# One expert slot picked inside attention and run unsplit during the routing

## The chip, the cores and the metric

The kernel runs on one core of one Trainium2 chip. The metric is the time of one execution on the device, in microseconds. Engines are named as in the profile: PE is TensorE's matrix product, PEld its weight load, DVE VectorE, ACT ScalarE, POOL GpSimd and SP the engine that issues most transfers.

## The reference, cut to what matters

```
q, k, v: (4, 8, 576, 64)                    # fp32
scores = rotate(q) @ rotate(k).T / sqrt(64)
attn_out = softmax(scores) @ v              # (4, 8, 576, 64)
x = attn_out.transpose(0, 2, 1, 3).reshape(2304, 512)

xn = x / (norm(x) + 1e-6);  en = emb / (norm(emb) + 1e-6)       # emb: (8, 512)
logits = xn @ en.T / tau
expert_idx = argmax(logits, axis=1)
gate_w = softmax(logits)[expert_idx]
for e in range(8):                          # w1: (8, 512, 1024), w2: (8, 1024, 512)
    mask = expert_idx == e
    out[mask] = gate_w[mask] * (relu(x[mask] @ w1[e]) @ w2[e])

h = out @ w_in                              # (512, 2048), float64
g = h - tanh(h)
return g @ w_out                            # (2048, 512), float64
```

## The kernel before, in words

**Stages.** The kernel has four stages, one after the other. Attention goes over 16 pairs of heads, four pairs to a batch. Then the rows are routed to the experts. Then the experts work on slots of rows. Then a dense layer of two products with a curve between works on six groups of 384 rows.

**Attention.** The order of attention's work is a list of some 1,200 steps written out by hand (`ORDER`, a string): `sm3.1` is "scores of pair 3, row block 1", `ld`, `ro`, `pp`, `ph`, `pl`, `sk` prepare q and k, `sx`, `se` are maximum and exponential, `tp`, `to` the transposes of the probabilities, `av` the product with v (L283), `xp` a product that gives normalised rows and logits (L293), `us` the logits of a batch, `sq` the squares of a row block and `st` the store of a batch's rows to `xscr` in HBM. The steps `cl` to `cs` convert the float64 `w_in` to fp32 beside attention (class `Convert`). Each engine has a queue of its own and takes its steps in the order of the list. The rope of q and k is POOL's, the products with v and `xp` are fp32 products, all other large products are of a high and a low fp32r part (three products in place of one).

**Routing** (`route`). When all logits are there, DVE makes a one-hot table `hot` of 8 experts by 20 row blocks (L491 to L500). Two products with a triangle and with ones count it (`cr`, L504). A chain of some 30 small DVE operations works out how many slots of 256 rows (big) or 128 rows (small) each expert takes, and the position of each row. ScalarE makes 8 of the 20 tables `row` by way of `lane` and `away` (L564 to L567), DVE the other 12, and 20 small products (`inv`, L574) turn positions into a list of rows per slot, `rt.idx`. Filler transposes (`idle`, L61, 64 and 24 of them) follow on TensorE after the counting and after the listing products. POOL then gathers the rows of the first slot from `xscr` (L830).

**Experts** (`Experts.run`, `block`, `small`). Slot 1 comes first, slots 2 to 7 follow always (`ALWAYS` = 8), further big slots and the small ones only where the registers say so, and slot 0 comes last. A block makes 8 groups of 12 products for the hidden rows (`hp`, L861), takes them through ReLU into a high and a low part (`ht`, L866 and L868), and makes two groups of 24 products for the output rows (`yp`, L882). Beside them ScalarE and DVE split the next weights into parts (`wh` and `wl`, `w1h` and `w1l`, L822 and L825). The rows of `y` are scattered to `yscr` in HBM. PSUM holds three banks each for `hp` and `yp`. The weights of a slot are loaded only where its expert differs from the one before. A list `steps` of bookkeeping (the scatter positions `rows`, the gates, 20 scatters of gates) is taken up at given places `f` of the blocks.

**Conversion of `w_out`.** In blocks 1 to 7, `Convert.step` runs at f = 1, 4 and 7 (blocks 1 to 4) or at f = 2 and 6: 18 steps, of which 16 load a piece. The clamp and the mask of a piece are DVE's (L742, L744), joining the halves is DVE's (L749), the addition is POOL's (L754), and a split writes two parts to HBM.

Of the kernel before, what the change touches and what calls it, by code (L numbers as in the profile page):

```python
# [30 lines left out]
ALWAYS, NBIG, NSMALL = 8, 12, 8  # L31
NSLOT = NBIG + NSMALL
R_FRESH, R_COUNT, R_SMALL, R_FIRST = 20, 40, 41, 42
# [5 lines left out]
PRE = 8  # L39
# [3 lines left out]
IDLE = (40, 64, 24)  # L43
# [20 lines left out]
def attention(tc, ctx, q, k, v, tables, emb, tau, ident, xscr, lg, us, ss, zero, conv):  # L64
    nc = tc.nc
    st = ctx.enter_context(tc.tile_pool(name="att_static", bufs=1))
    r_p = ctx.enter_context(tc.tile_pool(name="att_rope", bufs=1))
# [10 lines left out]
    tab = st.tile([128, 4, 5, D], F32, name="tab")  # L78
    raw = {n: [st.tile([128, 2, 5, D], F32, name=f"raw_{n}{i}") for i in range(RAW_BUFS[n])] for n in "qkv"}
# [37 lines left out]
    cv = Convert(tc, ctx, *conv, ROOM, zero)  # L117
# [9 lines left out]
    def rope(i, n):  # L127
        c = 0 if n == "q" else 2
        x = raw[n][i % RAW_BUFS[n]]
        if i == 0 or (i == 1 and n == "q"):  # L130
            eng = nc.vector
            w = pt_p.tile([128, 4, 2, S], F32, tag="pt", name="early", bufs=2).rearrange("p z a b -> p (z a b)")
            ra, rb = (w[:, 640 * y:640 * y + 640].rearrange("p (h r d) -> p h r d", h=2, r=5) for y in range(2))
        else:
            eng = nc.gpsimd
            ra, rb = (r_p.tile([128, 2, 5, D], F32, tag=y, name=y) for y in ("ra", "rb"))
# [8 lines left out]
        r = r_p.tile([128, 5, 2, D], F32, tag="rot" + n, name="rot" + n, bufs=2)  # L145
# [221 lines left out]
    for i in range(NP):  # L367
        nc.gpsimd.memset(ib[i][:, 128:144], 0.0)
        nc.gpsimd.tensor_copy(ib[i][:, 0:128], ident)

    do = dict(
        ld=load, ro=rope, pp=prep_pe, ph=prep_hi, pl=prep_lo, sk=stacks, sm=s_pe, sx=s_max, se=s_exp, tp=pt_pe, to=pt_out,
# [3 lines left out]
    turn_nothing(nc, ps_o, "o", ident, IDLE[0])  # L376
# [11 lines left out]
sa ro0.k sp ro0.q pp0.1 pp0.0 pp0.2 ph0.1 ph0.0 ph0.2 pl0.1 sd pl0.0 pl0.2 ld0.v ld1.k ld1.q cl0 ld2.q ld2.k ld1.v  # L388
cl1 ep2 ep3 sm0.0 ep0 sm0.1 ed3 sx0.0 ed0 ed2 sx0.1 se0.0 se0.1 ep1 sm0.2 sm0.3 sx0.2 ed1 sx0.3 se0.2 ro1.k se0.3
sm0.4 tp0.0.3 tp0.0.2 tp0.0.1 sm0.5 sx0.4 ro1.q sx0.5 to0.0.3 se0.4 to0.0.2 to0.0.1 tp0.0.0 pp1.1 to0.0.0 ph1.1  # L390
pp1.2 pp1.0 sm0.7 ph1.2 ph1.0 cc0 se0.5 sm0.6 pl1.1 pl1.2 pl1.0 sx0.7 cb0 sx0.6 cd0 cc1 se0.7 se0.6 ca0 ld3.k ld3.q
sk1.0 ro2.k ro2.q ce0 ro3.k ro3.q sm0.8 kp0 tp0.1.1 sm1.8 tp0.1.0 sx0.8 ko0 to0.1.1 sx1.8 to0.1.0 se0.8 up0.0 se1.8
uo0.0 tp0.1.2 sm1.0 up0.1 sm1.1 tp0.1.3 to0.1.2 sx1.0 sx1.1 to0.1.3 uo0.1 se1.0 se1.1 pp2.0 pp2.1 sm1.3 pp2.2 sm1.2
ph2.2 ph2.0 ph2.1 sx1.3 sx1.2 pl2.0 pl2.1 pl2.2 av0.0 up1.0 ld4.k cl2 sk1.1 ld4.q cs0 sk2.0 se1.3 se1.2 ca1 uo1.0
ca2 ao0.0 cc2 tp1.0.2 sm1.4 sm1.5 tp1.0.0 up1.1 av0.1 cb1 cd1 sx1.4 sx1.5 cb2 cd2 ce1 ro4.q ce2 ro4.k uo1.1 to1.0.2
se1.4 se1.5 to1.0.0 ao0.1 sm1.7 sm1.6 xp0.0 tp1.0.1 tp1.0.3 sx1.7 sx1.6 xd0.0 se1.7 se1.6 to1.0.3 to1.0.1 sm2.0
sm2.1 kp1 tp1.1.0 xp0.1 sx2.0 sx2.1 ko1 to1.1.0 xd0.1 cl3 ld5.q ld2.v sk2.1 cs1 cl4 ld5.k se2.0 se2.1 sm2.2 tp1.1.1
# [12 lines left out]
to4.1.2 to4.1.0 sx5.8 to4.1.1 sx5.0 up4.0 tp4.1.3 up4.1 se5.8 uo4.0 uo4.1 se5.0 ao3.1 sm5.2 kp4 to4.1.3 sx5.2 ko4  # L410
tp4.0.3 tp4.0.2 sm5.1 xp3.0 sx5.1 xd3.0 to4.0.3 se5.2 to4.0.2 se5.1 pp6.0 sm5.3 pp6.2 sm5.4 pp6.1 ph6.2 ph6.0 ph6.1
# [63 lines left out]
def route(tc, ctx, rt, cst, us, ps, idle):  # L475
# [23 lines left out]
    for b in range(B):  # L499
        v.memset(hot[64:128, :, 5 * b + 4], 0.0)  # L500
# [876 lines left out]
```

## Time and profile before

| What | Value |
|---|---|
| Median of 3 runs | 1028.66 us (1026.74 to 1039.12) |
| The profiled execution | 1032.44 us |
| Its span, first to last instruction | 1030.7 us |
| Mean granted TensorE clock | 0.977 of 2.4 GHz |
| PE busy | 977.6 us (95%) |
| DVE busy | 833.6 us (81%) |
| ACT busy | 652.0 us (63%) |
| POOL busy | 472.0 us (46%) |

Times within the kernel are microseconds from the start of the span. The mean length of a product says how long one is under way, not how far apart two of them follow: products are pipelined, so a distance is read from starts. In a timeline the bracket at the end of a line holds how long the engine stood idle before it and what released it. A granted clock of 1.00 is 2.4 GHz, of 0.50 it is 1.2 GHz.

### The profile page before, as it was taken

The page shows a single profiled execution, that of the slowest core. Times are in us where ns is not written, and L with a number is a line of the kernel's source. Part 1 is how long each engine was busy: PE and PEld are TensorE (multiplying, and loading weights), DVE is VectorE, ACT ScalarE, POOL GpSimd, SP SyncE. Part 2 cuts the span into 40 slices and gives each one's busy share as a digit, 9 for nine tenths or more (in the row PEclk, how much of TensorE's full clock was granted, in tenths as well). Part 3 has the DMA queues.
Part 4 walks back from the last instruction along what each step waited for, and adds up shares of the span by engine and source line. Part 5 has one row for each costly group of instructions (what it writes and reads, how often), then busy time and mean ns, then how long its engine had stood idle before and what let it go on. Part 6 is the DMA issues. An engine that isn't in the chain of part 4 may idle for free. (4 is left out here: it accounts for less than half of the span.)

```text
span 1030.7 us, 18144 instructions
## 1 busy us (share of the span) xinstructions
PE 977.6 (95%) x6004; PEld 854.2 (83%) x6004; DVE 833.6 (81%) x1472; ACT 652.0 (63%) x1466; POOL 472.0 (46%) x494
## 2 busy tenths in 40 slices
PE   8899999999996899999998799999999999999994
PEld 7787888888785788888986689999999999999993
DVE  6999888889677899898668659978878788788783
ACT  3677877877764577676566457655555656555661
POOL 5656656744301354544216435544444444443432
PEclk8899999999999899999999899999999999999998
DMA  6799889887714569979458397000100100000000
GB/s 192 170 225 233 209 225 218 223 200 179 188 46 144 200 173 286 316 198 232 133 180 271 133 296 277 31 31 1 31 31 1 59 4 31 31 1 1 31 1 31
DMA packets 98623, 140.75 MB, mean 137 GB/s; under 512 B 15945, under 2 KB 65097, under 8 KB 98002
## 3 DMA queue, kind: packets, MB, share of 16 engines
q1 hardware_dynamic: 92896, 123.40, 44.3%
q0 software_dynamic: 5440, 15.75, 4.5%
q8 instruction: 51, 0.84, 0.3%
q14 instruction: 58, 0.48, 0.2%
q10 hardware_dynamic: 178, 0.28, 0.1%
HBM read 101.11 MB, written 27.55 MB: 125 GB/s over the span
## 5 line engine op out<-in xcount | busy, mean ns | idle before, releaser
L1098 PE MATMUL dh<-yt,dwh 128*128 128x384 f32 x768 | 195.7, 335 | 0.0
L1098 PEld LDWEIGHTS dh<-yt,dwh 128*128 128x128 f32 x768 | 141.7, 188 | 8.3 <-DVE yt L1087 0.2
L1128 ACT ACTIVATE gh<-e 128x384 fp32r<-128x384 f32 x96 | 50.4, 525 | 144.5 <-DVE e L1121 144.5
L1108 POOL TENSOR_SCALAR e<-z 128x384 f32<-128x384 f32 x96 | 49.6, 517 | 189.8 <-DVE gl L1131 137.4
L236 ACT ACTIVATE p<-s,nm 128x576 f32<-128x576 f32 x144 | 106.5, 742 | 43.3 <-DVE nm L223 42.1
L1098 PE MATMUL dh<-yt,dwl 128*128 128x384 f32 x384 | 130.2, 339 | 0.0
L223 DVE TENSOR_REDUCE nm<-s 128x1 f32<-128x576 f32 x144 | 106.4, 752 | 26.7 <-PE s L218 22.7
L861 PE MATMUL hp<-xt,w1h 128*128 128x256 f32 x576 | 112.5, 297 | 14.4 <-DVE ht L868 8.6
L1155 PE MATMUL dy<-dwh,gh 128*128 128x512 f32 x288 | 114.8, 398 | 4.4 <-ACT gh L1128 2.6
L1155 PE MATMUL dy<-dwl,gh 128*128 128x512 f32 x288 | 114.5, 398 | 0.0
L1120 DVE SCALAR_TENSOR_TENSOR e<-q,e 128x384 f32<-128x384 f32 x96 | 111.0, 1156 | 3.4
L1155 PE MATMUL dy<-dwh,gl 128*128 128x512 f32 x288 | 113.7, 395 | 0.0
L861 PEld LDWEIGHTS hp<-xt,w1h 128*128 128x128 f32 x576 | 95.6, 201 | 17.6 <-DVE ht L868 10.1
L1109 POOL TENSOR_TENSOR e<-e,z 128x384 f32<-128x384 f32 x96 | 102.1, 1063 | 8.0
L1131 DVE TENSOR_TENSOR gl<-e,gh 128x384 fp32r<-128x384 f32 x96 | 54.3, 565 | 56.1 <-ACT gh L1128 55.5
L882 PE MATMUL yp<-wh,ht 128*128 128x512 f32 x288 | 90.9, 397 | 0.0
L218 PE MATMUL s<-ak 128*128 128x288 f32 x480 | 89.2, 314 | 1.2 <-ACT p L236 0.6
L861 PE MATMUL hp<-xt,w1l 128*128 128x256 f32 x288 | 85.0, 295 | 0.0
L825 DVE TENSOR_TENSOR wl<-raw,wh 128x512 fp32r<-128x512 f32 x84 | 65.0, 779 | 15.6 <-ACT wh L822 13.5
L218 PEld LDWEIGHTS s<-ak 128*128 128x128 f32 x480 | 67.6, 189 | 10.2 <-ACT p L236 4.5
L1121 DVE COPY_PREDICATED e<-m,t 128x384 f32<-128x384 int32 x96 | 72.3, 753 | 3.4
L249 PE MATMUL pt_ps<-ident,p 128*128 128x128 f32 x512 | 72.2, 278 | 0.5 <-DVE pt L125 0.4
(258 smaller groups left out, 2354.8 us busy)
## 6 DMA issues: line engine op xcount, KB each, us to landing
raw<-moe_w SPq DMA_DIRECT2D x176, 256.0 KB
ak<-hl SPq DMA_DIRECT2D x30, 448.0 KB
ak<-hl SPq DMA_DIRECT2D x30, 320.0 KB
c<-moe_w_in SPq DMA_DIRECT2D x16, 512.0 KB
c<-moe_w_out SPq DMA_DIRECT2D x16, 512.0 KB
raw_k<-k SPq DMA_DIRECT2D x16, 256.0 KB
raw_q<-q SPq DMA_DIRECT2D x16, 256.0 KB
raw_v<-v SPq DMA_DIRECT2D x16, 256.0 KB
```

What stands on the lines that cost most here:

```text
L218: nc.tensor.matmul(t[:, j, 0:HALF], lhsT=x[:, c:c + 128], rhs=x[:, k:k + HALF], start=(n == 0), stop=(n == len(parts) - 1))
L223: nc.vector.tensor_reduce(out=nm, in_=ps["s", i, u][:, :, 0:HALF], op=ALU.max, axis=AX.XY, negate=True)
L236: nc.scalar.activation(out=p.rearrange("p (j c) -> p j c", j=2), in_=ps.pop(("s", i, u))[:, :, 0:HALF], func=AF.Exp, bias=ps.pop(("nm", i, ...
L249: nc.tensor.transpose(t[:, r * 128:(r + 1) * 128], prob[i, r][:, 640 * h + 128 * kt:640 * h + 128 * kt + 128], ident)
L825: self.nc.vector.tensor_tensor(out=self.wl[m, c], in0=self.raw[m, c], in1=self.wh[m, c].bitcast(F32), op=ALU.subtract)
L861: nc.tensor.matmul(hp[:, 0:W], lhsT=a[1, f][:, kk * 128:(kk + 1) * 128], rhs=xt[b][:, kk, :], start=(n == 0), stop=(n == 3 * KD - 1))
L882: nc.tensor.matmul(yp, lhsT=ht[x][:, f, cs], rhs=b[2, f], start=(f == 0 and n == 0), stop=(f == KF - 1 and n == 2))
L1098: nc.tensor.matmul(h, lhsT=a[1, f][:, kk * 128:(kk + 1) * 128], rhs=self.yt[j][b][:, kk, :], start=(n == 0), stop=(n == 3 * KD - 1))
L1109: nc.gpsimd.tensor_tensor(out=e, in0=e, in1=z, op=ALU.mult)
L1120: v.scalar_tensor_tensor(out=e, in0=q, scalar=G_B, in1=e, op0=ALU.add, op1=ALU.mult)
L1121: v.copy_predicated(e, m.bitcast(I32), t)
L1155: self.nc.tensor.matmul(self.acc[j][a], lhsT=g[x][:, cs], rhs=b[2, f], start=(f == 0 and n == 0), stop=(f == self.KF - 1 and n == 2))
```

## The change

Attention's list now also holds the steps of one "early" slot. When the logits of the first three batches are there, DVE makes their part of the one-hot table, counts it, picks the expert with most rows and takes its first 256 rows (`mv14.0` to `mv14.12`, `mc14`, `mr14`, `ml14`). SP loads that expert's w1 and w2 (`mw15.0` to `mw15.15`), POOL gathers the rows (`mg14`), TensorE and ScalarE transpose them (`mp15`, `mo15`). The hidden and output products of this slot are unsplit fp32 products: two groups of hidden products stand before the counting product of the routing, six after it, one half of the output products before the transposes of the first block's rows, the other half after them. The filler transposes of the routing are gone. The rows taken are struck from `hot`, and `ALWAYS` falls from 8 to 7. The rest of the list is arranged anew from its first line on.

The weights and rows of the early slot lie in buffers that attention and the conversions use too: `rows` is one tile of 24 x 5 x 64 words that holds q, k, the rope's products and tables as views; `conv` and `cx` hold both conversions' pieces. In the conversion of `w_out` the clamp moves from DVE to POOL, the mask moves to the next step, and each of blocks 1 to 6 takes three steps. The PSUM pools after attention wait by tile.

```diff
-ALWAYS, NBIG, NSMALL = 8, 12, 8
+ALWAYS, NBIG, NSMALL = 7, 12, 8
+EARLY = (2, 6)
+EB = B - 1
+ET = 5 * EB
+A_ROPE, A_TAB, A_RAW, A_ROT, A_ROWS = 0, 4, 8, 16, 24
...
-    raw = {n: [st.tile([128, 2, 5, D], F32, name=f"raw_{n}{i}") for i in range(RAW_BUFS[n])] for n in "qkv"}
+    raw = {n: [early.pair(A_RAW, 2 * y + i) for i in range(RAW_BUFS[n])] for y, n in enumerate("qk")}
...
-            ra, rb = (r_p.tile([128, 2, 5, D], F32, tag=y, name=y) for y in ("ra", "rb"))
+            ra, rb = (early.pair(A_ROPE, y) for y in range(2))
...
+class Early:
+    def __init__(self, tc, ctx, rt, cst, us, xscr, yscr, w1, w2, ident):
...
+        self.rows = p.tile([128, A_ROWS, 5, D], F32, name="rows")
+        self.conv = p.tile([128, 6, 512], F32, name="conv")
+        cx = p.tile([128, 3, 513], F32, name="cx")
...
+    def steps(self, lg, bank):
...
+        def rows(i):
+            for t in range(ET):
+                g.tensor_scalar(out=row[t], in0=rt.iota, scalar1=lane[:, t:t + 1], scalar2=None, op0=ALU.is_equal)
+
+        def list_pe(i):
+            t = held["inv"] = bank()
+            for z in range(ET):
+                nc.tensor.matmul(t[:, 0:2], lhsT=row[z], rhs=col[:, z], start=(z == 0), stop=(z == ET - 1))
...
+    def up(self, f, ps):
+        nc = self.nc
+        hp = ps.tile([128, 512], F32, tag="h", name="eh")[:, 0:W]
+        for k in range(self.KD):
+            nc.tensor.matmul(
+                hp.rearrange("p (r d) -> p r d", r=4), lhsT=self.wv[0][f][:, k // 2, k % 2 * 128:k % 2 * 128 + 128],
+                rhs=self.x[:, 4 * k:4 * k + 4], start=(k == 0), stop=(k == self.KD - 1))
+        return lambda: nc.scalar.activation(out=self.h[f], in_=hp.rearrange("p (r d) -> p r d", r=4), func=AF.Relu)
+
+    def down(self, a, ps):
+        nc = self.nc
+        yp = ps.tile([128, 512], F32, tag="y", name="ey")
+        for f in range(self.KF):
+            nc.tensor.matmul(
+                yp.rearrange("p (h d) -> p h d", h=2), lhsT=self.h[f][:, 2 * a:2 * a + 2], rhs=self.wv[1][f],
+                start=(f == 0), stop=(f == self.KF - 1))
...
 def route(tc, ctx, rt, cst, us, ps, ps_h, early):
...
+    for x in pick(nc, rt, cst, us, sc, m2, ET, NT):
+        x()
+    for f in range(EARLY[0]):
+        early.up(f, ps_h)()
     cr = ps.tile([128, 512], F32, tag="t", name="cr")
...
-    idle(IDLE[1])
...
     nc.gpsimd.tensor_tensor(out=rank, in0=inc, in1=suf, op=ALU.add)
+    for f in range(EARLY[0], EARLY[1]):
+        early.up(f, ps_h)()
+    relus = [early.up(f, ps_h) for f in range(EARLY[1], Early.KF)]
...
     nc.scalar.activation(out=row[:, ac:], in_=away[:, ac:], func=AF.Relu, scale=-1.0, bias=1.0)
+    for x in relus:
+        x()
...
-    idle(IDLE[2])
...
     def clamp(self, n):
...
-        self.nc.vector.tensor_scalar(
+        eng = self.nc.gpsimd if self.late else self.nc.vector
+        eng.tensor_scalar(
             out=self.pad, in0=x.bitcast(F32), scalar1=least, scalar2=most, op0=ALU.max, op1=ALU.min)
+        if not self.late:
+            self.shift(n)
+
+    def shift(self, n):
+        x = self.xs[n % len(self.xs)]
         self.nc.vector.tensor_scalar(
             out=x, in0=self.pad.bitcast(I32), scalar1=0x07FFFFFF, scalar2=3, op0=ALU.bitwise_and, op1=ALU.logical_shift_left)
...
         if 0 < n <= len(self.jobs):
+            self.shift(n - 1)
             self.join(n - 1)
             self.add(n - 1)
...
-            if conv and f in ((1, 4, 7) if s <= 4 else (2, 6)):
+            if conv and f in (1, 4, 7):
                 conv.step()
...
-        if PRE == 8:
-            for a in range(2):
-                self.x_in(xg[a], a)
-            registers()
-        steps.insert(0, rows)
+        out = [early.down(0, self.ps_y)]
+        for a in range(2):
+            self.x_in(xg[a], a)
+        out[0]()
+        out.append(early.down(1, self.ps_y))
+        registers()
+        steps[0:0] = [out[1], rows]
...
-            self.block(s, None, conv, steps, range(6) if s == 1 else (1, 3, 5, 6))
+            self.block(s, None, conv, steps, range(7) if s == 1 else (1, 3, 5, 6))
```

The last lines of attention's list, before and after, show where the early steps stand:

```
...to15.1.2 xp14.0 up15.0 up15.1 av15.0 uo15.0 uo15.1 ao15.0 us2
xd14.0 xp14.1 av15.1 ao15.1 xp15.0 xp15.1 xd14.1 xd15.0 xd15.1 us3 us0 sq3.0 st3 sq3.1 sq3.2 sq3.3 sq3.4
```

```
...sk15.0 sk15.1 cs15 mw15.0 mw15.1 mw15.2 mw15.3 mw15.4 mw15.5 mw15.6 mw15.7 mw15.8 ld15.v mw15.9 mr14 sm14.7 xp12.1
...uo15.1 uo15.0 ao15.0 xd14.0 av15.1 xp14.1 ao15.1 xp15.0 xp15.1 xd14.1 xd15.0 xd15.1 us3 mv14.11 mv14.12 sq3.0
mw15.10 mw15.11 mw15.12 mw15.13 st3 mw15.14 mw15.15 sq3.1 sq3.2 sq3.3 sq3.4
```

## Rows read from the trace of the kernel before

**Rows 1.** The busy table of the page: engine, busy us, share, instructions.

```profile
PE 977.6 (95%) x6004; PEld 854.2 (83%) x6004; DVE 833.6 (81%) x1472; ACT 652.0 (63%) x1466; POOL 472.0 (46%) x494
```

**Rows 2.** Busy time by stretch: length, engines, granted clock, transfers' share, GB/s.

```profile
12.00:40.00 28.00, 23.65 (x127) 20.70 (x125) 22.74 (x41) 14.13 (x35) 19.58 (x16) 0.76 0.59 149
40.00:255.00 215.00, 213.44 (x1675) 175.74 (x1674) 189.86 (x381) 171.91 (x440) 131.74 (x108) 1.00 0.87 216
...
285.00:313.80 28.80, 28.75 (x223) 22.27 (x222) 18.42 (x44) 15.39 (x38) 0.78 (x6) 1.00 0.12 30
313.80:338.30 24.50, 14.49 (x119) 13.11 (x118) 19.56 (x60) 13.10 (x31) 4.86 (x6) 0.87 0.57 160
338.30:368.50 30.20, 27.41 (x154) 24.74 (x155) 28.13 (x87) 17.21 (x36) 9.82 (x8) 0.88 0.58 198
368.50:494.50 126.00, 120.02 (x762) 108.35 (x761) 109.60 (x183) 88.84 (x180) 61.73 (x53) 0.99 0.90 243
417.30:444.30 27.00, 25.09 (x154) 22.81 (x153) 23.40 (x39) 18.47 (x37) 13.37 (x11) 0.94 1.07 301
...
494.50:517.90 23.40, 23.40 (x154) 21.31 (x153) 16.82 (x30) 14.83 (x31) 6.20 (x5) 1.00 0.47 147
```

**Rows 3.** Timeline of the routing: start, length, engine, line, tiles, count, idle before.

```profile
318.42 0.43 PE L504 MATMUL cr<-hot,tri 128*128 128x160 f16 x2 [4.65 <-DVE hot L500]
...
318.64 8.70 PE L61 MATMUL idle<-ident 128*128 128x128 f32 x64
...
325.30 0.21 ACT L564 ACTIVATE lane<-ab 128x8 f32<-128x8 int32 x1 [5.59 <-DVE ab L555]
...
328.93 0.63 PE L574 MATMUL inv<-col,row 128*128 128x32 f16 x12 [0.34 <-DVE row L572]
...
334.81 0.66 PE L839 MATMUL xt_ps<-ident,xg 128*128 128x128 f32 x4 [2.59 <-DMA xg<-xscr,idx]
...
338.30 1.31 PE L861 MATMUL hp<-xt,w1h 128*128 128x256 f32 x2 [0.69 <-ACT xt L842]
```

**Rows 4.** The groups of instructions by line: the experts' products with the high part.

```profile
L861 PE MATMUL hp<-xt,w1h 128*128 128x256 f32 x576 | 112.5, 297 | 14.4 <-DVE ht L868 8.6 <-DVEq L1002 5.0 <-ACT xt L842 0.7
```

**Rows 5.** Timeline of PE, late attention: its fp32 products.

```profile
304.81 1.00 PE L293 MATMUL xo<-ib,ot 128*128 128x144 f32 x6
304.81 0.39 PE L293 MATMUL xo<-ib,ot 128*128 128x144 f32 x1
...
309.55 2.16 PE L283 MATMUL o<-pt,raw_v 128*64 128x288 f32 x16
311.54 0.66 PE L283 MATMUL o<-ptk,raw_v 128*64 128x288 f32 x4
```

**Rows 6.** Busy time by stretch, where the granted clock is half.

```profile
335.50:342.30 6.80, 4.94 (x20) 4.28 (x21) 4.40 (x25) 2.35 (x5) 5.34 (x4) 0.50 0.71 224
...
349.10:352.50 3.40, 3.40 (x16) 3.32 (x17) 3.28 (x9) 3.39 (x9) 0.47 (x1) 0.50 0.18 28
```

**Rows 7.** Timeline of block 1: the conversion's first piece, and the wait for DVE.

```profile
348.46 0.66 ACT L733 ACTIVATE cx<-c 128x512 f32<-128x512 f32 x1 [4.57 <-DMA c<-moe_w_out]
...
348.95 0.68 PE L861 MATMUL hp<-xt,w1h 128*128 128x256 f32 x2 [2.65 <-DVE ht L868]
```

**Rows 8.** Timeline of block 4, and two groups by line: splits, additions, clamps.

```profile
423.68 2.29 DVE L825 TENSOR_TENSOR wl<-raw,wh 128x512 fp32r<-128x512 f32 x1
424.13 1.28 POOL L754 TENSOR_TENSOR cx<-cx,cu 128x512 int32<-128x512 int32 x1
...
426.23 0.68 DVE L825 TENSOR_TENSOR wl<-raw,wh 128x512 fp32r<-128x512 f32 x1
426.36 0.39 PE L861 MATMUL hp<-xt,w1h 128*128 128x256 f32 x1 [1.91 <-DVE ht L868]
...
L742 DVE TENSOR_SCALAR pad<-cx 128x513 f32<-128x513 f32 x16 | 10.8, 678 | 1.8 <-ACT cx L733 1.8
L900 POOL TENSOR_SCALAR w1h<-raw 128x512 fp32r<-128x512 f32 x4 | 4.2, 1058 | 0.0
```

More of the change, by code (lines that the diff above doesn't have):

```diff
@@ L144, in rope @@
             )
-        r = r_p.tile([128, 5, 2, D], F32, tag="rot" + n, name="rot" + n, bufs=2)
+        r = early.flat(A_ROT, 2 * "qk".index(n) + i % 2).rearrange("p (r h d) -> p r h d", r=5, h=2)
         eng.tensor_tensor(out=r.rearrange("p r h d -> p h r d"), in0=ra, in1=rb, op=ALU.add)
@@ L369, in attention, with bank @@
         nc.gpsimd.tensor_copy(ib[i][:, 0:128], ident)
+    def bank():
+        return ps_t.tile([128, 512], F32, tag="t", name="early")
     do = dict(
-        ld=load, ro=rope, pp=prep_pe, ph=prep_hi, pl=prep_lo, sk=stacks, sm=s_pe, sx=s_max, se=s_exp, tp=pt_pe, to=pt_out,
+        **early.steps(lg, bank), ld=load, ro=rope, pp=prep_pe, ph=prep_hi, pl=prep_lo, sk=stacks, sm=s_pe, sx=s_max, se=s_exp, tp=pt_pe, to=pt_out,
         kp=key_pe, ko=key_out, up=tail_pe, uo=tail_out, av=av_pe, ao=av_out, xp=out_pe, xd=out_rows, us=logits, st=store_x,
@@ L393 @@
[L393 to L397, printed above, removed]
@@ L476, in route @@
+def route(tc, ctx, rt, cst, us, ps, ps_h, early):
     nc = tc.nc
@@ L562, in route @@
     lane = tl("lane", [128, NT])
-    away = tl("away", [128, NT, 128], F16)
+    away = row
     nc.scalar.activation(out=lane[:, ac:], in_=ab[:, 1, ac:], func=AF.Copy)
@@ L658, in rows @@
         v.tensor_reduce(out=pf, in_=pos.rearrange("p e t -> p t e"), op=ALU.add, axis=AX.X)
-        v.tensor_copy(rt.row, pf)
+        v.tensor_tensor(out=rt.row, in0=pf, in1=rt.base, op=ALU.add)
     return registers, rows
@@ L964, in small, with run @@
             in_=y, in_offset=None, bounds_check=YROW - 1)
-    def run(self, registers, rows, steps, net):
+    def run(self, registers, rows, steps, net, early):
         nc, tc, rt, conv = self.nc, self.tc, self.rt, self.conv
@@ L1272, in moe_kernel @@
     rt.row = const.tile([128, NT], I32, name="row")
+    rt.tri = const.tile([128, 2, 128], F16, name="tri")
+    rt.iota = const.tile([128, 128], F16, name="iota")
+    rt.hot = const.tile([128, E, NT], F16, name="hot")
+    rt.tok = const.tile([128, NT], F32, name="tok")
+    rt.base = const.tile([128, NT], F32, name="base")
+    rt.first, rt.lost = (const.tile([128, 1], F32, name=n) for n in ("first", "lost"))
+    rt.idxe, rt.toe = (const.tile([128, 2], I32, name=n) for n in ("idxe", "toe"))
     xscr = dram.tile([NROW, DM], F32, name="xscr")
```

403 lines of the change are left out of this document (274 added, 129 removed).

## The prediction

> **What bounds the kernel now.** I read the busy table first: TensorE has work in 95% of the span [rows 1], so what counts is where it does not, and which of its work goes away. The table by stretch comes next [rows 2]. From 40 us to the end of attention TensorE is busy 99% of the time or more: attention is bound by TensorE, apart from its first 28 us (4.35 us without work, mean clock 0.76). Then 24.5 us of routing follow, in which TensorE is "busy" for 14.49 us because filler transposes stand there, 64 of them in one row of 8.70 us and 24 more after the listing product [rows 3]; the chain that sets this stretch is DVE's. Block 1 takes 30.2 us, block 7, with no table or conversion work beside it, 23.4 us, all of it TensorE at full clock. The five blocks between take 126.0 us, the longest of them 27.0.
>
> **Does a slot go away?** Routing the reference's own rows gives 974, 149, 597 and 584 rows to experts 1, 2, 5 and 6 and none to the others. That is nine slots of 256 and two of 128, as the trace has it: 576 products with the high part are nine times 8 x 8 [rows 4]. Expert 1 has its 974 rows in the first three batches, so it is the one picked; 718 remain, three slots in place of four. So eight full slots and two small ones run, and one block goes. I price it at the barest one: **-23.4 us** [rows 2].
>
> **The price of the unsplit products.** The nearest rows are attention's fp32 products. The regrouping product (128x128 weights, 144 columns) leaves two records each; six records end 1.00 us after the first starts and one alone lasts 0.39 us [rows 5], so they follow each other every (1.00 - 0.39)/5 = 0.122 us. One product is 0.244 us for 144 columns, 1.69 ns a column. The product with v has 64-wide weights: 16 records start within 311.54 - 309.55 = 1.99 us [rows 5], 0.249 us per product of 288 columns, 0.86 ns a column. The early slot loads 128x128 weights, so I take the first. Up: 8 x 4 products of 256 columns at 0.434 us = 13.9 us. Down: 2 x 8 of 512 at 0.868 us = 13.9 us. Sum 27.8 us; 14.2 us by the other row.
>
> **How much of it the routing hides.** (1) Attention's last product ends at about 313.4; the first two up groups (8 x 0.434 = 3.5 us) end near 317, before the one-hot table for which the counting product waits until 318.42 [rows 3]. That wait stays: the last maximum and the table are now made for one batch, but nine small DVE operations of the early slot stand before them. (2) The other six groups, 10.4 us, run from 318.9 to 329.3 in the fillers' place. ScalarE's lane copy, at 325.30 now, stands behind the ReLU of the sixth group (318.9 + 6.9, then 0.4): about 326.5, +1.2 us. The eight tables that ScalarE makes behind it are ready 1.2 us later, and so the listing product (its last twelve are at 328.93 now [rows 3]), the index and the gather: about +1.3 us. (3) The first half of down (6.9 us) fills 330.8 to 337.7, while the first gathered rows, on TensorE at 334.81 now [rows 3], land at 336.1 and the second ones some 1.7 us later. (4) Their transposes take until 338.9, and the second half of down (6.9 us) covers their copies: block 1 starts at 345.8 in place of 338.30, **+7.5 us**. If the products went at the rate of the 64-wide row, the ups would delay nothing and one half of down (3.6 us) would be left: about +2. If one half-clock stretch of 3.4 us, like that from 349.1 [rows 6], falls in, +1.7 more.
>
> **Block 1.** Its 30.2 us are 23.4, a wait of 2.65 us for DVE [rows 7], 4.0 us at half clock at its head and 3.4 us at half clock from 349.1 [rows 2, 6]: 2.0 and 1.7 us. After the change TensorE works without a gap up to it, so I drop the 2.0. The register work moves off it too, into the second half of down, but the rest of the bookkeeping and a conversion step stay on DVE in front of the splits, so a wait of about 2 us is left, and half of the 1.7. About 26.3: **-3.9 us**; between -6.8 (the bare block) and 0. The conversion's first load now waits until the second half of down has read its buffer, and SP's queue holds block 1's loads behind it. At present ScalarE waits 4.57 us for that load while the expert weights fill the queues [rows 7]; after the change these have landed, and the wait should be under 1 us.
>
> **The conversion steps.** All 18 still run, three in each of six blocks in place of 3, 3, 3, 3, 2, 2, 2. Sixteen of them lose one DVE operation (0.68 us) to POOL, whose nearest price is 1.06 us [rows 8]. What speaks against this is in the trace: the DVE split wl takes 0.68 us, but 2.29 us where POOL's addition of 1.28 us runs, and TensorE then stands for 1.91 us [rows 8]; beyond five bare blocks, the five from 368.5 take 126.0 - 117.0 = 9 us. At present the clamp and the mask separate the addition from the next split on DVE; afterwards the mask comes first and the split follows at once, and POOL holds two operations instead of one. I take half a microsecond more per block, **+2.5 us** for blocks 2 to 6, from -2 (DVE's relief wins) to +8 (two collisions in each, and a half-clock stretch). The Trainium skill (SBUF — State Buffer, "Who interferes with whom") says that a DVE instruction with two SBUF inputs and a GpSimd instruction that reads SBUF exclude each other for a whole instruction. The trace agrees, with 2.29 us against 0.68; by that rule taken to the letter, rival B below happens.
>
> **Attention.** Added on TensorE: two counting products (0.43 us), 15 listing products (12 take 0.63 us, so 0.8) and eight transposes (0.66 us for four, at most 1.2) [rows 3]: **+2.3 us**, all on the bound engine. DVE gets some 27 operations; at the 0.33 us of routing (19.56 us for 60) that is at most 9 us where DVE is busy 18.42 of 28.8 us [rows 2]: hidden, at the cost of short waits. POOL's 15 comparisons and two gathers fall where it is busy 0.78 us. The early weights, 4.2 MB and 24 issues on SP, go out after the last pair's stacks, where the queues are busy 12% of the time, ahead of the last v load; they need some 14 us at the 301 GB/s of a loaded block [rows 2]. Hidden; each microsecond by which they came late would delay the counting product behind the ups. The order of attention is another list throughout: in its first 28 us, with waits and half clock, this can give or take 4 us. I give -4 to +6.
>
> The dense layer, the small slots and block 0 keep their work, and the removed fillers cost nothing, since they hide under DVE's chain. **Sum:** -23.4 + 7.5 - 3.9 + 2.5 + 2.3 = -15.0 us. Against the profiled execution (1032.44 us, 1.7 of them outside the span) that is 1017.4; that execution lies 3.8 us above the median of the runs, 1028.66, and the comparison will be of medians: **1014 us**.
>
> **Rivals.** A: the rest of the waits goes too. POOL's clamp collides with nothing, blocks 1 to 6 run at 24.2 us each (145.2 in place of 156.2), and attention's own waits absorb its additions: -23.4 + 7.5 - 11.0 + 1 = -26, 1003 us; with half of this, 1008. For it: DVE loses 16 operations of 0.68 us. Against: the collisions are in the trace already.
> B: the collision becomes the rule. In each of six blocks the two steps in the up half hold a split for 1.2 us more, of which one is paid already: +7.2 us, and two half-clock stretches after such waits, +3.4, in place of the +2.5: 1022 us. For it: TensorE feels nearly the whole of a long split. Against: it has three PSUM banks of slack.
> C, slower than before: q and k, the rope's products and tables now lie in one tile. If order were kept by the whole tile rather than by the rows that are touched, a load of q or k would wait for the rope before it. Some 15 pairs pass between 40 and 313.8 us, 18 us each, and POOL, with the ropes, has work for 131.74 of 215 us there, 11 us a pair [rows 2]; once rope and load in a row exceed the pair, each of 15 pairs pays the excess, and from 1.0 us (15 us) on the change loses. At 2 us a pair: 1014 + 30 = 1044. Against: the views are separate boxes.
> D: the picked rows take no slot away, or the early rows are run twice. Then the 23.4 stays: 1037. The counts speak against it.
>
> **How the numbers follow.** Forecast 0.52 (1008 to 1019), A 0.22, B 0.19, C 0.05, D 0.02. The range takes A in to its end and B with its clock: **1003 to 1025**. Two per cent, about what a measurement of this kernel tells from no change, is 20.6 us: under 1008.1 lie A's part beyond half and a tail of the forecast, 0.23; over 1049 a tail of C, 0.03; 0.74 within.
>
> **What would show it.** Right: 512 products with the high part in place of 576; 64 + 32 records of unsplit products, 0.217 and 0.434 us apart; no fillers after attention; block 1 first at 346 to 349; attention's end at 314 to 317. Wrong: ups waiting for weights or rows before the counting product; wl splits of over 1.4 us in more than five places; POOL or SP waits inside attention that were not there; a half clock in the ups.

## The result and the profile after

The changed kernel takes **1040.77 us** (median of 20 executions, 1034.03 to 1047.4), the kernel before 1034.51 us beside it (20 executions, 1026.74 to 1039.21): a ratio of 1.0067, with an interval of 1.0044 to 1.009. That is slower by 0.7%, and 16 us above the top of the predicted range.

The busy table of the page, after: TensorE has 119 instructions fewer and is yet busy 1.4 us longer, and POOL is busy 43 us longer [rows 1].

```profile
PE 979.0 (94%) x5885; PEld 843.8 (81%) x5885; DVE 822.4 (79%) x1463; ACT 641.1 (62%) x1450; POOL 515.4 (50%) x524
```

Busy time by stretch, after; columns as in [rows 2]. The first three rows are late attention, then come the routing, block 1, and blocks 2 to 6.

```profile
285.00:290.00 5.00, 2.86 (x25) 2.62 (x23) 4.06 (x7) 2.88 (x8) 0.38 (x1) 1.00 0.81 211
290.00:304.20 14.20, 8.42 (x41) 7.26 (x42) 1.82 (x4) 3.19 (x8) 10.65 (x17) 0.52 0.82 218
304.20:327.90 23.70, 23.16 (x183) 17.54 (x182) 12.06 (x34) 10.48 (x25) 0.00 (x0) 1.00 0.13 46
327.90:358.70 30.80, 28.95 (x127) 19.39 (x125) 24.41 (x92) 16.48 (x41) 6.64 (x7) 1.00 0.66 204
358.70:390.50 31.80, 26.66 (x155) 22.72 (x153) 20.36 (x53) 16.68 (x36) 15.95 (x11) 0.95 0.45 148
390.50:529.90 139.40, 124.25 (x762) 107.83 (x762) 117.11 (x177) 88.55 (x182) 93.95 (x68) 0.96 0.84 228
```

In attention TensorE stands idle for 7.9 of the 19.2 us from 285 to 304.2 (5.00 - 2.86 and 14.20 - 8.42), and from 290 on the granted clock is about half (0.52). Blocks 2 to 6 take 139.4 us where they took 126.0 [rows 2], and POOL has 93.95 us of work in them, 61.73 before. The account between the two profiled executions, from the starts of each stage's first product or last copy of y (these two executions lie 9.9 us apart, the medians 6.3):

| Stage | before, us | after, us | difference | forecast |
|---|---|---|---|---|
| attention, to its last product | 313.5 | 327.6 | +14.1 | +2.3 |
| from there to block 1's first product | 24.8 | 31.1 | +6.3 | +7.5 |
| block 1 | 30.2 | 31.8 | +1.6 | -3.9 |
| blocks 2 to 6 | 126.0 | 139.4 | +13.4 | +2.5 |
| the block that goes | 23.4 | - | -23.4 | -23.4 |
| last full block, small slots, block 0 | 87.4 | 88.5 | +1.1 | 0 |
| dense layer | 425.5 | 422.3 | -3.2 | 0 |
| sum | | | +9.9 | -15.0 |

**Where attention stands.** Timeline after: DVE's last lanes, SP's store of the last `w_in` piece, POOL's tables, TensorE's listing products.

```profile
280.32 0.18 DVE L613 SCALAR_TENSOR_TENSOR lg<-lg 128x20 f32<-128x20 f32 x1
...
284.71 1.49 SPq L989 DMA_DIRECT2D win<-cx  x1
...
289.62 8.71 POOL L622 TENSOR_SCALAR cx<-iota,lg 128x128 f16<-128x128 f16 x15 [30.50 <-DMA win<-cx]
...
290.30 0.18 PE L627 MATMUL early<-lg,cx 128*128 128x2 f16 x1 [2.44 <-POOL cx L622]
...
298.39 0.18 PE L627 MATMUL early<-lg,cx 128*128 128x2 f16 x1 [0.39 <-POOL cx L622]
```

The lanes are ready at 280.5 us, and POOL is free. But the tables are written into `cx[0]` and `cx[1]`, and `cx[0]` holds the last converted piece of `w_in` until its store has landed. So POOL begins at 289.62, and 15 tables take 8.71 us. TensorE takes its queue in order: the 15 listing products of 0.18 us wait for one table each, with the last pair's work behind them. TensorE waits 7.9 us there, works 2.8 us on tiny products, and the clock is about half until 304.2.

**The routing.** Timeline of TensorE after; it answers to [rows 3]. The early slot's products stand where the fillers stood, and from 327.69 to block 1 the only waits are 1.45 and 0.40 us.

```profile
327.69 3.62 PE L684 MATMUL eh<-rows,conv 128*128 128x256 f32 x16
332.76 0.30 PE L724 MATMUL cr<-hot,tri 128*128 128x160 f16 x2 [1.45 <-DVE hot L503]
...
344.15 0.36 PE L798 MATMUL inv<-col,row 128*128 128x32 f16 x8 [0.40 <-ACT row L789]
344.37 3.68 PE L693 MATMUL ey<-rows 128*128 128x512 f32 x8
...
358.66 0.80 PE L1094 MATMUL hp<-xt,w1h 128*128 128x256 f32 x2
```

**The blocks.** Groups by line, after; then the chain of waits of blocks 2 to 6 (engine, line, releaser: us in total, times, longest); then DVE and POOL in block 2.

```profile
L1094 PE MATMUL hp<-xt,w1h 128*128 128x256 f32 x512 | 95.3, 288 | 10.0 <-DVE ht L1101 3.7 <-ACTq L1233 3.4 <-DVE xt L1076 2.8
...
L969 POOL TENSOR_SCALAR rows<-cx 128x513 f32<-128x513 f32 x16 | 35.7, 2231 | 3.8 <-issue 3.8
```

```profile
ACT rows L994 <- POOL cx L986: 32.9, 10, 5.7
...
PE xt_ps L1072 <- DMA xg<-xscr,idx: 8.3, 3, 3.5
...
DVE cx L976 <- POOL rows L969: 3.1, 5, 0.8
```

```profile
405.95 2.49 DVE L1058 TENSOR_TENSOR wl<-raw,wh 128x512 fp32r<-128x512 f32 x1
...
406.58 1.30 POOL L986 TENSOR_TENSOR cx<-cx,rows 128x512 int32<-128x512 int32 x1
407.84 2.41 POOL L969 TENSOR_SCALAR rows<-cx 128x513 f32<-128x513 f32 x1
```

The clamp takes 2231 ns on POOL, not 1058 [rows 8]. Its own result is hardly waited for (3.1 us). But the addition behind it comes late: ScalarE's split waits 32.9 us for it, the gather of the next rows is late by 8.3 us on TensorE, and the addition now falls beside a split. The split that starts at 405.95 ends 0.56 us after the addition. In blocks 2 to 6, 10 of the 83 splits that DVE makes take over 1.4 us, each of them beside an addition; before, 4 of 80.

### The profile page after: what moved, and what is told of

Read it like the earlier page. It is cut to its first block, busy times and chain, and to the rows that moved or that the text cites. A ratio compares the mean times of both kernels' runs of the same rounds, so it can differ in the third digit from the quotient of the medians.

```text
span 1040.5 us, 17919 instructions
## 1 busy us (share of the span) xinstructions
PE 979.0 (94%) x5885; PEld 843.8 (81%) x5885; DVE 822.4 (79%) x1463; ACT 641.1 (62%) x1450; POOL 515.4 (50%) x524
## 5 line engine op out<-in xcount | busy, mean ns | idle before, releaser
L241 ACT ACTIVATE p<-s,nm 128x576 f32<-128x576 f32 x144 | 106.3, 741 | 40.1 <-DVE nm L228 36.1
L1094 PE MATMUL hp<-xt,w1h 128*128 128x256 f32 x512 | 95.3, 288 | 10.0 <-DVE ht L1101 3.7
L223 PE MATMUL s<-ak 128*128 128x288 f32 x480 | 91.4, 318 | 2.1 <-ACT p L241 1.8
L1115 PE MATMUL yp<-wh,ht 128*128 128x512 f32 x256 | 86.9, 415 | 5.4 <-DVE ht L1101 4.3
L1094 PEld LDWEIGHTS hp<-xt,w1h 128*128 128x128 f32 x512 | 81.0, 194 | 12.9 <-DVE ht L1101 4.4
L1094 PE MATMUL hp<-xt,w1l 128*128 128x256 f32 x256 | 73.0, 285 | 0.0
```

Of the source, the lines that this page charges most:

```text
L223: nc.tensor.matmul(t[:, j, 0:HALF], lhsT=x[:, c:c + 128], rhs=x[:, k:k + HALF], start=(n == 0), stop=(n == len(parts) - 1))
L241: nc.scalar.activation(out=p.rearrange("p (j c) -> p j c", j=2), in_=ps.pop(("s", i, u))[:, :, 0:HALF], func=AF.Exp, bias=ps.pop(("nm", i, ...
L1094: nc.tensor.matmul(hp[:, 0:W], lhsT=a[1, f][:, kk * 128:(kk + 1) * 128], rhs=xt[b][:, kk, :], start=(n == 0), stop=(n == 3 * KD - 1))
L1115: nc.tensor.matmul(yp, lhsT=ht[x][:, f, cs], rhs=b[2, f], start=(f == 0 and n == 0), stop=(f == KF - 1 and n == 2))
```

## The experiments

### Undoing the two suspects, one at a time and together

Theory: the buffer of the tables and the clamp on POOL, each for itself, cost what the account shows. Rival: what is late next takes the gain. The four kernels of this group ran on one chip, with the kernel before at a median of 1031.86 us beside them; gains are therefore told as distances from it. The changed kernel lies 6.3 us above the kernel before (1040.77 against 1034.51).

**Tables in other buffers.**

```diff
-        row = [self.cx[t // 8][:, t % 8 * 64:t % 8 * 64 + 64].bitcast(F16) for t in range(ET)]
+        row = [self.cx[1 + t // 8][:, t % 8 * 64:t % 8 * 64 + 64].bitcast(F16) for t in range(ET)]
```

> The changed kernel with one edit: POOL's 15 early tables stand in the second and third of the three small conversion buffers, free since two earlier stores, and no longer in the first, whose store is the last to land. Listing theory (attention's +14.1 us is TensorE standing in order behind tables that could not start before that store landed, and the half clock after it): the tables start near 281 in place of 289.6 and end near 289, the wait of TensorE for them falls from 7.9 us over 15 times to under 2, attention's last product ends near 316 to 318 in place of 327.7, and the run is 10 to 12 us shorter than the changed kernel, about 1029. Rival (the new order or the shared tile stalls attention elsewhere): the tables start earlier, but attention still ends after 324 and the run stays within 4 us of 1041.

Measured 1027.77 us, 4.1 under the kernel before, ratio 0.9968 (0.994 to 0.9997): a gain of 10.4. The wait of POOL and the stretch from 285 us to attention's end, now at 316.1:

```profile
POOL cx L622 <- DVE lg L613: 21.6, 1, 21.6
```

```profile
285.00:316.20 31.20, 29.82 (x248) 23.88 (x248) 17.98 (x44) 16.65 (x41) 6.93 (x10) 1.00 0.61 170
378.20:514.10 135.90, 122.12 (x762) 108.25 (x762) 117.97 (x177) 89.09 (x182) 94.01 (x68) 0.96 0.84 235
```

POOL now waits for the lanes and no longer for the store; the half clock is gone, and attention ends 11.5 us earlier, 2.6 us after the kernel before, where 2.3 were forecast. Blocks 2 to 6 (second row) keep most of their excess: 135.9 us, 126.0 before.

**Clamp back on DVE.**

```diff
-        eng = self.nc.gpsimd if self.late else self.nc.vector
-        eng.tensor_scalar(
+        self.nc.vector.tensor_scalar(
             out=self.pad, in0=x.bitcast(F32), scalar1=least, scalar2=most, op0=ALU.max, op1=ALU.min)
-        if not self.late:
-            self.shift(n)
+        self.shift(n)
...
         if 0 < n <= len(self.jobs):
-            self.shift(n - 1)
```

> The changed kernel with one edit undone: the clamp of the w_out conversion is DVE's again and the mask follows it in the same step; three steps a block stay. Clamp theory (16 clamps of 2.2 us on POOL hold up its queue and the splits on DVE): blocks 2 to 6 fall from 139.3 us to 124 to 129, block 1 by 2 to 4 us, the small slots come back to 32.4 from 36.6 or not at all; the run is 12 to 18 us shorter than the changed kernel, about 1026. Rival (three steps in every block, beside the new buffers, are the cause): blocks 2 to 6 stay above 135 us and the run within 5 us of 1041.

Measured 1029.75 us, 2.1 under the kernel before, ratio 0.9987 (0.9957 to 1.0017): a gain of 8.4, less than the 12 to 18 expected. Blocks 2 to 6 fall as far as expected, block 1 by 1.4 us (31.8 to 30.4) in place of 2 to 4:

```profile
389.50:516.40 126.90, 119.82 (x762) 106.97 (x762) 110.19 (x186) 89.42 (x181) 65.27 (x54) 0.99 0.88 250
```

**Both.**

> Both edits of the two other kernels together. If the two causes are separate the gains add: 22 to 30 us under the changed kernel, 1011 to 1019, and 15 to 23 us under the kernel before. If one only uncovers the other (the blocks start earlier but then wait for transfers), the sum is under 18 us.

Measured 1017.33 us, 14.5 under the kernel before, ratio 0.987 (0.9811 to 0.993). The gain is 20.8 us, a little under the 22 to 30 expected, where the two alone make 18.7: with intervals of some 3 to 6 us on each ratio, nothing shows that either is taken back by what is late next. Blocks 2 to 6 take 124.7 us; block 1 still takes 33.2, which is the next question.

```profile
348.80:382.00 33.20, 26.26 (x157) 23.74 (x156) 23.82 (x60) 16.95 (x36) 9.75 (x8) 0.90 0.52 175
382.00:506.70 124.70, 119.36 (x763) 105.40 (x762) 110.60 (x186) 89.56 (x182) 65.18 (x54) 1.00 0.90 254
```

**The clamp's move alone, in the kernel before.**

```diff
     def clamp(self, n):
...
-        self.nc.vector.tensor_scalar(
+        eng = self.nc.gpsimd if self.late else self.nc.vector
+        eng.tensor_scalar(
...
+        if not self.late:
+            self.shift(n)
+
+    def shift(self, n):
...
+            self.shift(n - 1)
             self.join(n - 1)
```

> The kernel before with one part of the change alone: the clamp of the w_out conversion on POOL, the mask at the next step. Clamp theory: block 1 to block 6 lose some 10 to 15 us, a little less than in the changed kernel because blocks 5 and 6 have two steps and not three; the run is 8 to 15 us above the kernel before. Rival (the clamp costs only in the changed kernel's arrangement): within 4 us of the kernel before, or faster by DVE's relief of 16 x 0.68 us.

Measured 1043.12 us, ratio 1.0125 (1.006 to 1.019): the move loses 11.3 us without any of the rest. Blocks 2 to 6 take 132.0 us in place of 126.0, and block 1 36.1 in place of 30.2.

### Why block 1 stays long

In the kernel with both repairs, block 1 from its first product at 348.8 us: ScalarE and DVE, and TensorE behind them.

```profile
355.93 0.67 ACT L959 ACTIVATE cx<-conv 128x512 f32<-128x512 f32 x1 [3.31 <-DMA conv<-moe_w_out]
...
356.64 0.69 DVE L968 TENSOR_SCALAR rows<-cx 128x513 f32<-128x513 f32 x1 [3.35 <-ACT cx L959]
...
362.16 0.18 DVE L882 TENSOR_TENSOR row<-pf,base 128x20 int32<-128x20 f32 x1
...
363.33 0.79 PE L1091 MATMUL hp<-xt,w1h 128*128 128x256 f32 x2 [6.94 <-DVE ht L1098]
```

SP issues the conversion's load at 349.46, when the early slot's last products have read the buffer, and ScalarE can use it at 355.93. DVE's clamp waits for that, the positions' small operations (357.96 to 362.3) stand behind the clamp, and the next split and `ht` behind those. TensorE has three banks of slack, waits 6.94 us, and the clock is half from 361.4 to 368.3. Two theories: the load, or the positions.

**The first conversion step later**, on top of both repairs:

```diff
-            if conv and f in (1, 4, 7):
+            if conv and f in ((4, 6, 7) if s == 1 else (1, 4, 7)):
```

> The kernel with both repairs (tables in the other buffers, clamp on DVE), with the conversion's first step of block 1 at f = 4 and its others at f = 6 and 7. There block 1 takes 33.1 us: ScalarE stands for 3.3 us before the first size operation for the conversion's load, DVE's clamp waits for that, and behind the clamp stand the scatter positions (4.3 us of small operations) and the splits; TensorE waits 6.9 us for ht and then runs at half clock for 6.9 us. Theory L (the load that waits for its buffer is the cause): ScalarE's wait is under 1 us, TensorE's wait for ht falls below 3.5 us, block 1 takes 25 to 28 us, total 1009 to 1013. Rival P (the positions' 4.3 us on DVE are the cause): TensorE still waits 5 us or more, block 1 31 to 33 us, total 1015 to 1019.

Measured 1014.23 us, ratio 0.9846 (0.9779 to 0.9912).

**And the positions in three pieces**, `rows` being now a tuple of three functions:

```diff
-        steps[0:0] = [out[1], rows]
+        steps[0:0] = [out[1], *rows]
...
-            self.block(s, None, conv, steps, range(7) if s == 1 else (1, 3, 5, 6))
+            self.block(s, None, conv, steps, range(8) if s == 1 else (1, 2, 3, 5, 6) if s == 2 else (1, 3, 5, 6))
```

> As the run before it in this group, and the scatter positions cut into three pieces at f = 1, 2 and 3, with the gate's steps one or two places later. Theory L: the load was the cause, so block 1 gains no more than 1 us over that run. Rival P: block 1 falls by a further 3 us or more, to 25 or 26 us, because no more than 2 us of small operations then stand in front of a split. Total 1007 to 1012 by either; the step between the two runs decides.

Measured 1011.96 us, ratio 0.9807 (0.9754 to 0.9861). Block 1 of the first, then of the second:

```profile
348.90:376.70 27.80, 25.61 (x157) 23.05 (x155) 23.57 (x60) 17.20 (x36) 9.96 (x8) 0.94 0.62 204
```

```profile
350.70:375.80 25.10, 24.25 (x155) 21.35 (x153) 21.66 (x55) 17.05 (x35) 10.64 (x8) 1.00 0.57 194
```

33.2, 27.8, 25.1: the place of the first conversion step made 5.4 us of block 1 and the positions 2.7, so both theories hold for block 1, in this order; the limit of 1 us that the load's theory set for the second step is broken. But the second step does not shorten the kernel: block 2, 23.9 us in the first of the two runs, takes 27.9 in the second, where a small operation on DVE lasts 1.86 us beside POOL's addition and TensorE then waits 2.7 us. The medians differ by 2.3 us, within their spread, and the profiled execution of the second is the longer one.

### Through what POOL's clamp acts

The clamp on POOL changes three things at once: POOL's queue, the order of the steps, and what runs beside DVE. The next kernels start from the one with both repairs, so the order of steps is DVE's.

**A clamp on POOL that nothing reads**, boxed like the true one, then flat:

```diff
         self.nc.vector.tensor_scalar(
             out=self.pad, in0=x.bitcast(F32), scalar1=least, scalar2=most, op0=ALU.max, op1=ALU.min)
+        if self.late:
+            self.nc.gpsimd.tensor_scalar(
+                out=self.spare, in0=self.free, scalar1=least, scalar2=most, op0=ALU.max, op1=ALU.min)
```

> The kernel with both repairs, and behind each of the 16 clamps of DVE a clamp of the same shape on POOL, between two buffers that nothing else uses at that time: POOL's queue is as full as in the changed kernel, but nothing waits for the result. Theory Q (the time on POOL's queue, through the addition, the scatters and the gathers behind it, or through DVE's accesses beside it): blocks 2 to 6 take 133 us or more in place of 124.7, and the total is 1024 to 1030. Rival D (the clamp's place in the chain size, clamp, mask, join, add, split made the waits): blocks 2 to 6 stay at 124 to 128 us, total 1015 to 1020. The operation itself should take 1.9 to 2.4 us, as in the changed kernel.

> As the run before it in this group, with the output of the unread POOL operation flat (513 words in a row) in place of three boxes of 171. If the boxes made the changed kernel's clamp twice as long as the nearest row of the kernel before (1.06 us), it falls to about 1.1 us, and the total lies between that run and the kernel with both repairs, 1018 to 1024. If the pair of operations, maximum and minimum, made it, it stays at 1.9 to 2.4 us and the total equals that run's within 3 us.

Measured 1027.84 us (0.9965, 0.9933 to 0.9996) and 1031.66 us (1.0001, 0.9973 to 1.003). The boxed one's group and blocks 2 to 6, and the flat one's group:

```profile
L971 POOL TENSOR_SCALAR rows<-rows 128x513 f32<-128x513 f32 x16 | 36.6, 2290 | 0.1
```

```profile
380.20:517.60 137.40, 124.26 (x762) 109.78 (x761) 123.38 (x187) 89.75 (x182) 95.78 (x67) 0.96 0.80 236
```

```profile
L971 POOL TENSOR_SCALAR rows<-rows 128x513 f32<-128x513 f32 x16 | 35.7, 2232 | 0.1
```

Work on POOL that nobody waits for costs 12.7 us in blocks 2 to 6 (137.4 against 124.7), no less than the true clamp, 11.2 (135.9 against 124.7). The clamp's place in the chain is not the cause of that, and the boxes are not the cause of its length: flat it takes 2232 ns too. What differs from the row of 1058 ns [rows 8] is the pair of operations, maximum and minimum here, multiplication and addition in that row. That row also writes fp32r, but this is not it: in the dense layer POOL's multiplication and addition into fp32 takes 515 ns for 384 columns.

**POOL's time alone.** In place of the unread clamp, a power of 12 columns:

```diff
+        if self.late:
+            if n == 0:
+                self.nc.gpsimd.memset(self.free, 0.5)
+            self.nc.gpsimd.tensor_tensor(out=self.spare, in0=self.free, in1=self.free, op=ALU.pow)
```

> The kernel with both repairs, and behind each of DVE's 16 clamps a power of 12 columns on POOL that nothing reads: by the row of the gates' power (20 columns, 3.6 us) it should hold POOL for some 2.2 us, as the unread clamp did, but touch 12 columns of the buffers in place of 513. Theory T (POOL's time is what counts: the addition, the gathers and the scatters behind it come late): blocks 2 to 6 take 133 to 139 us, as with the unread clamp (137.4), total 1025 to 1031. Rival M (what counts is that POOL's long operations and DVE's splits hold each other up over the buffers): blocks 2 to 6 stay at 124 to 129 us, total 1015 to 1020, and the splits wl keep their mean of 0.78 us in place of 0.86.

Measured 1027.17 us, ratio 0.9952 (0.9928 to 0.9975). The power took 2676 ns. Blocks 2 to 6, and two splits with POOL's addition and power beside the second:

```profile
380.90:516.70 135.80, 123.29 (x762) 107.55 (x762) 122.19 (x189) 88.95 (x181) 96.65 (x67) 0.97 0.78 234
```

```profile
395.32 0.69 DVE L1059 TENSOR_TENSOR wl<-raw,wh 128x512 fp32r<-128x512 f32 x1
...
396.25 2.50 DVE L1059 TENSOR_TENSOR wl<-raw,wh 128x512 fp32r<-128x512 f32 x1
...
396.89 1.31 POOL L988 TENSOR_TENSOR cx<-cx,rows 128x512 int32<-128x512 int32 x1
398.15 2.77 POOL L973 TENSOR_TENSOR rows<-rows 128x12 f32<-128x12 f32 x1
```

So it is POOL's time, not the data that the added work moves. Yet the splits are long again: 12 over 1.4 us in blocks 2 to 6, each of them beside POOL's *addition*, none beside the power alone; 5 in the kernel with both repairs. There 19 of DVE's clamps and masks have an addition beside them and keep 0.67 to 0.69 us. A later queue moves the additions out of DVE's clamp and mask and into its splits.

**No addition on POOL, but a full queue**, with 18 columns in the power:

```diff
-        self.nc.gpsimd.tensor_tensor(out=x, in0=x, in1=self.u.pop(n), op=ALU.add)
+        eng = self.nc.vector if self.late else self.nc.gpsimd
+        eng.tensor_tensor(out=x, in0=x, in1=self.u.pop(n), op=ALU.add)
```

> As the kernel with the unread power on POOL, but the addition of the conversion is DVE's too (it rounds there, so the low words of w_out's parts are not the reference's) and the unread power has 18 columns, some 4 us: POOL's queue is as full as with clamp and addition, but no conversion work of POOL stands beside DVE's splits and ScalarE waits for no addition of POOL. Theory A (the late additions: they fall beside the splits, 17.6 us of excess in blocks 2 to 6 of the run with 12 columns, and ScalarE waits 29.8 us for them): blocks 2 to 6 fall from 135.8 us to 124 to 129, total 1015 to 1021, splits back to a mean of 0.70 us, although the gathers are as late as before. Rival G (the late gathers: TensorE waited 5.9 us for the next block's rows and then ran at half clock): blocks 2 to 6 stay at 131 to 138, total 1023 to 1030, with a wait of 5 us or more for xg.

Measured 1021.42 us (1016.59 to 1025.45), ratio 0.9909 (0.9882 to 0.9937), the kernel before at 1030.41. Blocks 2 to 6 of the profiled execution, the fastest of the nine, with POOL busy for 90.67 us of them:

```profile
378.40:505.30 126.90, 118.43 (x763) 106.38 (x762) 114.29 (x200) 90.53 (x182) 90.67 (x53) 0.99 0.81 247
```

With POOL nearly as busy (96.65 us with the smaller power) and no addition on it, no split of these blocks lasts 0.8 us, and 8.9 of the 11.1 us that the power had added are gone. But the profiled execution of the run with the smaller power was the slowest of its ten, so this difference is an upper end; by the medians, each against the kernel before beside it, it is 4.2 of 9.8. The additions are the larger part in the one view and rather less than half in the other. The median, 1021.42 us, falls between the two theories' ranges. What the late gathers (2.9 us of waiting here) and DVE's 16 more operations make of the rest stays open. The Trainium skill (SBUF — State Buffer, "Who interferes with whom") lets a DVE instruction with two SBUF inputs contend with a GpSimd instruction that reads SBUF. The additions agree, with 2.50 us against 0.69. The power reads two inputs as well, but of few columns, and the 39 splits that it touches take 0.68 to 0.75 us in this run. Beside the unread clamp alone, which reads 513 columns, 21 splits took 0.68 to 1.09 us, so the hold-up seen beside the additions is not there for every operation of POOL.

**Splitting a piece one step later**, clamp on POOL and tables moved, with a fourth buffer:

```diff
-        if 1 < n < len(self.jobs) + 2:
-            self.split(n - 2)
+        lag = 3 if self.late else 2
+        if lag <= n < len(self.jobs) + lag:
+            self.split(n - lag)
```

> The changed kernel with the tables in the other buffers (clamp still on POOL), and each conversion piece split one step later, with a fourth buffer for it: ScalarE no longer meets an addition that POOL has not yet made. If the way from POOL's queue to TensorE leads through ScalarE's in-order wait for the addition (32.9 us of waits in the changed kernel), blocks 2 to 6 fall from 143.0 us in that kernel's run to 128 to 134, total 1014 to 1020. If it leads through the gathers and through DVE operations held up beside POOL, they stay within 4 us of 143 and the total at 1025 to 1030, although ScalarE's waits for the addition fall under 5 us.

Measured 1033.44 us, ratio 1.0027 (0.9998 to 1.0056), against 1027.77 without it: no gain, if anything a loss. (Blocks 2 to 6 of the kernel it starts from took 135.9 us, as its row above shows; the 143.0 in the expectation is wrong.) Here they take 136.2. But the test does not decide: ScalarE's wait for the addition did not go, it moved to the next use of the fraction's buffer, of which there are two:

```profile
ACT rows L963 <- POOL cx L986: 12.9, 6, 3.7
...
ACT rows L963 <- POOL rows L986: 8.1, 2, 5.6
```

### A version that beats both

All four edits (tables, clamp, first step, positions), with the gate's last DVE step of block 2 at f = 2:

```diff
-range(8) if s == 1 else (1, 2, 3, 5, 6) if s == 2 else (1, 3, 5, 6)
+range(8) if s == 1 else (2, 3, 4, 5, 6) if s == 2 else (1, 3, 5, 6)
```

> Tables in the other buffers, clamp on DVE, first conversion step of block 1 at f = 4, positions in three pieces, and the gate's last DVE step of block 2 one place later (at f = 2). In the run with the pieces at f = 1 to 3, a DVE operation of that step lasted 1.86 us beside POOL's gathers and addition (0.18 us in others), TensorE waited 2.7 us, and block 2 took 27.8 us with a half clock behind it. Expected: blocks 1 and 2 at 25 and 24 us, total 1007 to 1012; if that delay comes from the conversion step and not from the place of the gate's step, block 2 stays at 27 us and the total at 1011 to 1014.

Measured **1011.74 us** (1009.58 to 1015.52), ratio 0.9809 (0.9772 to 0.9845): 1.9% under the kernel before, and by the two ratios 2.6% under the changed one (0.9809 / 1.0067 = 0.9744). Block 1 and blocks 2 to 6:

```profile
349.80:374.90 25.10, 24.17 (x156) 21.27 (x154) 21.69 (x55) 17.02 (x35) 10.63 (x8) 1.00 0.56 198
374.90:501.60 126.70, 119.63 (x762) 107.16 (x762) 115.71 (x191) 89.81 (x181) 64.29 (x54) 0.99 0.91 256
```

Block 2 took 26.9 us, so the place of that step was not what lengthened it, as the other branch of the expectation has it. POOL's addition now falls beside a split, which lasts 2.12 us; TensorE waits 1.8 us, and from 382 to 390 the mean granted clock is about 0.8. Blocks 1 and 2 together take 52.0 us, with the first step's move alone 51.7: the positions in pieces are not shown to gain anything.

## Why the prediction was wrong

**The slot** went as priced: 512 products with the high part. **The unsplit products** were priced right: 16 records of a hidden group span 3.62 us and 8 of an output group 3.68, which is 0.216 and 0.44 us from one to the next for 0.217 and 0.434 predicted. **The routing** came out at +6.3 us for +7.5, with the full clock kept throughout.

**Attention: the step that failed is "POOL's 15 comparisons and two gathers fall where it is busy 0.78 us".** The busy share was right, and POOL was indeed idle. What was not asked is in which buffer the tables stand and when it comes free: the wait on a store to HBM is in no row of before, but the diff puts the tables into `cx`. I costed 0.8 us of products on the bound engine as if their input were there; they waited 7.9 us for it, took 2.8, and the clock fell. Measured +14.1 us for +2.3. With other buffers attention ends 11.5 us earlier, at +2.6.

**Blocks 2 to 6: the step that failed is the clamp's price of 1.06 us, and the +2.5 us that rest on it.** The nearest row was of another pair of operations, and the true price is 2.23 us. The upper bound of +8 counted two collisions in each block. That mechanism, rival B's, is there (10 long splits for 4 before), but I let only the clamp and DVE's order decide it. Sixteen times 2.23 us in POOL's in-order queue also moves the gathers (8.3 us on TensorE) and the additions that ScalarE's split waits for. That POOL's added time is the cause is shown, by the clamp's return and by the unread work; how it divides between the long splits, ScalarE's wait and the gathers is not. Measured +13.4; with both repairs -1.3.

**Block 1: "the wait should be under 1 us" failed**, at 3.37 us in the changed kernel (SP's issue of the load, then ScalarE's first use):

```profile
359.29 0.81 SPq L954 DMA_DIRECT2D conv<-moe_w_out  x2
365.84 0.67 ACT L959 ACTIVATE cx<-conv 128x512 f32<-128x512 f32 x1 [3.37 <-DMA conv<-moe_w_out]
```

I saw the load wait for its buffer but took the weights to have landed by then. They had not: from issue to use, 6.55 us, the transfers' share is 0.83, at 306 GB/s. TensorE waits 2.40 us for the `ht` behind it. A second wait, 1.8 us in all, stands behind POOL: ScalarE waits 8.41 us for gates that follow an addition and a clamp in POOL's queue, and this the forecast did not have. Forecast -3.9 us; +1.6 measured. With both repairs and the first step later it is -2.4; the -5.1 with the positions in pieces is lost again in block 2.

**What I costed at nothing** moved by little: the last full block, the small slots and block 0 by +1.1 us, the dense layer by -3.2. That layer starts with TensorE busy for 28.19 of its first 30 us before and, with both repairs, 30.00; I looked no further into it.

Rivals: A did not happen; the best version, 20.2 us under the kernel before, comes near its half (1008). C's stall did not come: between 40 and 255 us TensorE works 212.85 of 215 us, 213.44 before [rows 2]. Of D nothing was seen. The two failed steps together are 20.8 us; without them the kernel lies 14.5 us under the one before, where the forecast said 15.0. That these two agree so well is partly luck: block 1's miss, some 7 us there, is made up by blocks 2 to 6 (3.8) and the dense layer (3.2).

## What to carry to other kernels

An idle engine hides added work only if its input and its output buffer are free by then: for each tile that an edit reuses, look up who held it last, and if that was a transfer, take its landing time. Price an operation by a row with the same operations on the same engine, not only the same shape, and then read what stands behind it in that engine's queue: unread work on POOL cost as much as work that was needed. Where one instruction lengthens another, look at which two meet: the same addition was free beside a mask (0.69 us) and cost 1.8 us beside a split (2.50 against 0.69).

## What the runs showed of the hardware that was not expected

POOL takes, in the mean, 2.23 to 2.29 us for a maximum and a minimum over 128x513 fp32, boxed or flat (kernel after and the two unread clamps), and 0.73 to 1.06 us for a multiplication and an addition over 128x512 (kernel before and the kernel with both repairs); DVE takes 0.68 us for the former. The Trainium skill (GPSIMD Engine Reference, "Elementwise — side-by-side cycle accounting") has measured times for an addition of two fp32 tensors, GpSimd's 1.96 times VectorE's; for a maximum and a minimum over one tensor the ratio here is 3.3. A power of 18 columns holds POOL for 3.42 us in the mean, and no split beside it lasts over 0.75 us. And a DVE operation of 20 columns, 0.18 us elsewhere, lasted 1.86 us beside POOL's gather and addition in the kernel with the positions in pieces, in block 2:

```profile
382.64 1.86 DVE L920 TENSOR_SCALAR g<-g 128x20 f32<-128x20 f32 x1
```
